# A gated mix of sliding-window attention and a mixer MLP on one Trainium2 core: the probabilities' block split in two, tokens loaded a unit earlier, five MLP steps moved ahead of the last P times V, and weight loads moved into the attention's end

## The chip, the core and the metric

The kernel runs on one NeuronCore of one Trainium2 chip. A core has five engines, each with an instruction queue of its own that it works off in order: TensorE (PE; its weight loads are shown apart as PEld), VectorE (DVE), ScalarE (ACT), GpSimd (POOL) and SyncE (SP). SP only issues DMAs here, and ACT issues some too. The engines meet at semaphores. Matmuls write PSUM, which has eight banks of 2 KB a partition; everything else lives in SBUF (128 partitions) or in HBM.

The metric is the device time of one execution in microseconds (us), the median of several runs. An execution's profile shows the span from the first to the last instruction of the program, which is about 2 us less.

## What is computed

`x` is (2048, 512), float32. Two branches are mixed by a gate of one number per token:

```python
g = _sigmoid((x * gate_w).sum(-1, keepdims=True))
# A: attention, H = 32 heads of 16, causal, window W = 256
q, k, v = split(x @ wqkv)
scores = jnp.einsum("bhqd,bhkd->bhqk", q, k) * (Dh ** -0.5)
mask = (idx[:, None] - idx[None, :] >= 0) & (idx[:, None] - idx[None, :] < W)
p = _softmax(jnp.where(mask, scores, -1e9), axis=-1)
a = einsum("bhqk,bhkd->bhqd", p, v) @ wo
# B: per-token MLP, F = 1792
y = _layernorm(x)
b = _gelu(y @ w1 + b1) @ w2 + b2
out = g * a + (1 - g) * b
```

The products are made in three terms from a high and a low part of each operand (`split`, `lo_part`), so each float32 weight block is loaded raw, copied to its high part and subtracted to get its low part: one copy on ACT or DVE and one subtraction on DVE or POOL.

## The kernel before

There are three stages, each one stream of work on PE with the other engines beside it. Nothing is scheduled by a planner while it runs: the order is written out, by a table of units in the first stage, by a string of 1,202 letters in the second, by a loop in the third. `tick` counts steps, and `after(k, fn)` emits `fn` k steps later; what is emitted earlier stands earlier in its engine's queue. A tile takes one of the buffers of its tag, and an instruction waits until the buffer's last user is done.

**Stage 1: projections (0 to about 149 us).** 48 units, each a matmul group of 12: Q or K of a head group for 512 tokens (`qk_unit`, L290) or V of 128 tokens (`v_unit`, L320). `at(n, fn)` puts other work ahead of unit n's matmuls. Q and K go through HBM: `qk_out` stores their high and low parts from `t` tiles, `load_stacks` (L331) loads the score operands of four heads into `qk`. `gaps` (L203) fills rows of the HBM copy. `stat_unit(i)` loads 128 tokens from `xa` (L441); after 3 steps ACT makes their sums (`sums`, L444 and L445), after 4 DVE makes the gate's dot product (`dot`, L448). `s_pair` (S; L344) makes a block of scores for the row maximum, two heads at a time; DVE masks it (L353) and reduces it (L354). In this stage two PSUM buffers (`ps_x`) are kept for it. The first ten blocks of queries are done here, two pairs a block. The pool `work` holds, in order of first use, `gws` and `waste` (2 KB a partition each), four `wv` (4 KB) and fourteen `t` (2 KB).

**Stage 2: attention, with MLP1 in its gaps (about 149 to 498 us).** `work` is closed and opened again on the same bytes. Its first tile is the block `five` of probabilities (tag `p`, L596); nine `t` follow. `p_tile` hands out seven slots in turn: five in this block, two in tiles of the pool `x`. Eight passes of four heads run over 16 blocks of 128 keys. The string `ORDER` gives the steps: T is `st_pair` (L399, scores of two heads; L401, the exponential on ACT, written to a slot; L403, masks on POOL), S is `s_pair` for the row maximum of what comes later, P is `pv` (L418, probabilities times V for 256 queries; the result is copied out by ACT or DVE at L425 and stored), and f is `fill`: one step of `mlp1_unit`, two matmuls (L621). A unit of MLP1 has 24 steps; there are 28 units, 672 steps, and the string has 647. Its result is copied out by ACT and stored to `hp`. Four PSUM banks `b0` to `b3` go round among T, S and P, one of them held by the open MLP1 unit. `block(p, kb)` runs at each first T of a key block and issues loads; in the last pass it starts the load and split of the first W2 blocks (`early_w2`) and of the first two tiles of MLP1's result (`load_h`).

After the string, the gelus of the two early tiles go to ACT, the last P is run, the pools are opened again (44 `t`), and a loop works off the MLP1 steps that are left.

**Stage 3: MLP2 and the attention's output (about 504 us to the end).** For each 512 tokens and each of 14 blocks of F, `mlp2` makes 12 matmuls (L832). `load_w2` (L650) and `load_h` (L674) run six items ahead; gelu is at L677, its high part at L681. At item 4 of the first 512 tokens, `attn_out` starts: it loads the row sums `su` (L783), takes their reciprocal on DVE (L788), stores them, loads the unscaled attention and the factors (L795, L796), scales (L799) and multiplies by Wo (L811; `load_wo`, L656).

Of the kernel before, what the change touches and what calls it, by code (L numbers as in the profile page):

```python
# [20 lines left out]
D = 512  # L21
# [6 lines left out]
C = 512  # L28
# [27 lines left out]
def gated_mix_kernel(ctx, tc: tile.TileContext, xt, x2, wq0, wqk, wv, wo, xa, gw, w1, w2, b1, b2, out):  # L56
    nc = tc.nc
    dve, act, pool, pe, sp = nc.vector, nc.scalar, nc.gpsimd, nc.tensor, nc.sync
# [5 lines left out]
    def nm(s):  # L64
        uid[0] += 1
        return f"{s}_{uid[0]}"
# [10 lines left out]
    def get(key, tag, bufs, shape, dt=F32):  # L77
        return left[key].tile(list(shape), dt, name=nm(tag), tag=tag, bufs=bufs)
# [3 lines left out]
    def t2(dt=F32, shape=(128, 512)):  # L82
        return get("work", "t", nt[0], shape, dt)
# [19 lines left out]
    def two():  # L103
        if not ring:
            return ps("x", (128, 2, 512))
        ring.append(ring.pop(0))
        return ps(ring[-1], (128, 2, 512))

    def small(tag, bufs, shape, dt=F32):
        return consts.tile(list(shape), dt, name=nm(tag), tag=tag, bufs=bufs)  # L110

    def view(t, *ap, off=0):
        return bass.AP(tensor=t.tensor, offset=t.offset + off, ap=[list(x) for x in ap])

    def f32(t):
        return t.bitcast(F32)

    def lo_part(lo, src, hi, eng=dve):
        eng.tensor_tensor(out=lo, in0=src, in1=f32(hi), op=ALU.subtract)  # L119
# [7 lines left out]
    def after(k, fn):  # L127
        todo.setdefault(step[0] + k, []).append(fn)
# [43 lines left out]
    def x8():  # L172
        return get("x", "x8", 10, (128, 2048), F32R)
# [4 lines left out]
    def split(w, raw, both=False):  # L178
        if both:
            dve.tensor_copy(w[:, 0], raw)  # L180
        else:
            copy(w[:, 0], raw)
        lo_part(w[:, 1], raw, w[:, 0])
# [142 lines left out]
    def load_stacks(p, a, n):  # L326
        g, j = divmod(p, 2)
        held_cols[p] = a + n
        for t in (1, 0):
            src = view(qkd[g, t], [S, 98], [100 * S, 2], [1, n], off=4 * j * 50 * S + a)  # L330
            sp.dma_start(f32(qk[14:112, 2 * t:2 * t + 2, a:a + n]), f32(src))  # L331
# [3 lines left out]
    def s_pair(p, qb, pr):  # L335
        if qb == 0 and pr == 0:
            mxs[p] = small("mx", 2, (128, 2, 2, NB))
        assert qb * 128 < held_cols[p]
        n = min(qb + 1, 3) * 128
        t0 = qb * 128 + 128 - n  # L340
        o = two()
        for e in range(2):
            r, k = ((0, 62), (64, 112))[e]
            pe.matmul(o[:, e, :n], qs[pr][r:k, qb * 128:qb * 128 + 128], ks[pr][r:k, t0:t0 + n],  # L344
                      start=True, stop=True)
        m = mxs[p][:, pr, :, qb]
        if qb < 2:
            for e in range(2):
                sc = small("scr", 2, (128, 256), BF16)
                dve.tensor_tensor_reduce(out=sc[:, :n], in0=o[:, e, :n], in1=wide[:, 256 - n:], scale=1.0, scalar=NEG,  # L350
                                         op0=ALU.add, op1=ALU.max, accum_out=m[:, e:e + 1])
        else:
            dve.copy_predicated(o[:, :, :128], tri, o[:, :, 256:384])  # L353
            dve.tensor_reduce(m, o[:, :, :256], mybir.AxisListType.X, ALU.max)  # L354
        if pr and qb % 4 == 3:
            put_max(p, qb - 3)
# [82 lines left out]
    def stat_unit(i):  # L439
        s = t2()  # L440
        sp.dma_start(s, xa[i])  # L441

        def sums():
            act.activation(waste, s, AF.Copy, scale=-1.0 / D, accum_out=mv[:, i, 0:1])  # L444
            act.activation(waste, s, AF.Square, bias=mv[:, i, 0:1], accum_out=mv[:, i, 1:2])  # L445

        def dot():
            dve.scalar_tensor_tensor(out=s, in0=s, scalar=1.0, in1=gws, op0=ALU.mult, op1=ALU.mult,  # L448
                                     accum_out=z[:, i:i + 1])

        after(3, sums)
        after(4, dot)

    def stat_end(half):
        ve = small("ve", 2, (128, NB // 2))
# [92 lines left out]
    def at(n, fn):  # L548
        plan.setdefault(n, []).append(fn)
# [5 lines left out]
    for i in range(4):  # L555
        at((3, 5, 6, 8)[i], lambda i=i: pool.memset(vs[:, 4 * i:4 * i + 4], 1.0))
    at(2, masks)
    at(10, load_consts)
    for g in range(NG):
        at((8, 16, 20, 24)[g], lambda g=g: gaps(g))  # L560
    for c in range(NCH):
        at((11, 20, 29, 44)[c], lambda c=c: load_stacks(0, c * C, C))
    for i in range(NB):
        at(10 + i, lambda i=i: stat_unit(i))
    at(21, lambda: stat_end(0))
    at(29, lambda: stat_end(1))
    at(25, lambda: load_mr(0))
# [6 lines left out]
    at(38, lambda: load_w1(0, dve))  # L574
    at(41, lambda: load_w1(1, dve))
    for qb in range(NB - LAG):
        at((17, 19, 21, 23, 25, 27, 29, 31, 34, 37)[qb], lambda qb=qb: [s_pair(0, qb, pr) for pr in range(2)])
    for n, u in enumerate(units):
        if n > 1:
            tick()  # L580
# [12 lines left out]
    extra = [f32(x8())[:, :1536].rearrange("p (h n) -> p h n", h=4) for _ in range(2)]  # L593
    np_ = [0]

    five = get("work", "p", 1, (128, 5, 4, 384))  # L596

    def p_tile():
        n = np_[0] % 7
        np_[0] += 1  # L600
        return extra[n // 4] if n in (2, 5) else five[:, n - n // 3]

    late = []

# [38 lines left out]
    def load_w2(f):  # L643
        if f % 2 == 0:
            w2t.append(x8())
            if f == 2:
                spare.append(x8())
        w = w2s[f] = w2t[-1][:, f % 2 * 2 * C:f % 2 * 2 * C + 2 * C].rearrange("p (k n) -> p k n", k=2)
        raw = t2()
        sp.dma_start(raw, w2[f])  # L650
        return lambda both=False: split(w, raw, both)

    def load_wo(dt):
        w, raw = wt(), t2()
        wos[dt] = w
        sp.dma_start(raw, wo[dt])  # L656
        return lambda both=False: split(w, raw, both)

    def early_w2():
        for n in range(4):  # L660
            def go(n=n):
                fn = load_w2(n)
                after(2, lambda: fn(True))
            after(1 + n, go)

    def early_wo(a):
        fns = [load_wo(a), load_wo(a + 1)]
        after(4, lambda: [fn() for fn in fns])

    hs = {}  # L670

    def load_h(c, f):
        s = t2()
        sp.dma_start(s, hp[c, f])  # L674

        def gelu():
            act.activation(s, s, AF.Gelu_apprx_tanh, bias=b1s[:, f:f + 1])  # L677

        def parts(dst=None):
            h, l = dst or (t2(F32R), t2(F32R))  # L680
            dve.tensor_copy(h, s)  # L681
            lo_part(l, s, h)
            hs[c, f] = h, l

        return gelu, parts
# [10 lines left out]
    def block(p, kb):  # L696
        tick()
        if kb % 2 == 0:
            if kb and p + 1 < 8:
                load_stacks(p + 1, kb * 128 - 256, 256)  # L700
            if not kb and p:
                load_stacks(p, S - 256, 256)
        if p in (0, 2, 4) and kb % 2 == 0:
            double(p // 2 + 1, kb // 4, 1 - kb // 2 % 2)
        if p == 7 and kb == LAG:
            early_w2()
        if p == 7 and kb == 12:
            early.extend(load_h(0, f) for f in range(2))

    early = []  # L710
    spot[0] = 0
# [4 lines left out]
    def run(order):  # L716
        for a in order:
            spot[0] += 1
            for fn in soons.pop(spot[0], []):
                fn()  # L720
            flush()
            if a == "T":
                p, kb, pr = lt.pop(0)
                if not pr:
                    block(p, kb)
                st_pair(p, kb, pr)
            elif a == "S":
                s_pair(*ls.pop(0))
            elif a == "P":
                pv(*lp.pop(0), not ls)  # L730
            else:
                fill()

    run(ORDER)
    flush()
    for f, (gelu, _) in enumerate(early):
        gelu()
# [17 lines left out]
    waiting = {}  # L755
    for f in range(2, 4):
        waiting[0, f] = load_h(0, f)
    for f in range(4, 6):
        waiting["w", f] = load_w2(f)
    for f in range(4, 6):  # L760
        waiting[0, f] = load_h(0, f)
    for f in range(4, 6):
        waiting.pop(("w", f))()
    while jobs or cur[0]:
        fill()
    flush()
# [3 lines left out]
    low, high = {"o0": 1, "o1": 1, "a4": 1, "a5": 1}, {f"a{i}": 1 for i in range(4)}  # L770
    open_psum(*((low, high) if "b0" in used else (high, low)))
    b2s = get("work", "b2s", 1, (128, D))
    sp.dma_start(b2s, view(b2, [0, 128], [1, D]))

    after(1, gate)
    for n in range(2):
        after(1 + 2 * n, lambda n=n: early_wo(2 * n))
    us = {}

    def attn_out(c):  # L780
# [64 lines left out]
    for n in range(len(seq)):  # L845
        tick()
        for k in (n + 6,):
            c, f = item(k)
            if f >= 0:
                if c == 0 and f > 3:  # L850
                    waiting["w", f] = load_w2(f)
                waiting[c, f] = load_h(c, f)
        c, f = item(n + 1)
        if ("w", f) in waiting and c == 0:
            waiting.pop(("w", f))()
        if (c, f) in waiting:
            waiting[c, f][1]()
        if item(n + 2) in waiting:
            waiting[item(n + 2)][0]()
        c, f = seq[n]  # L860
        if f == (4 if c == 0 else 2):
            attn_out(c)
        mlp2(c, f)
# [49 lines left out]
```

## Time and profile before

| what | us |
|---|---|
| three runs | 708.22, 712.19, 714.32 |
| median | 712.19 |
| profiled execution, its own time | 709.97 |
| its span | 708.0 |
| TensorE busy in it | 690.4 |

The page's first part gives, for each engine, busy time, share of the span and instructions. The granted clock of TensorE is 0.998 of full speed over the span. The page's slices of the span show DMA busiest in the first stage (eight or nine tenths) and least at the very end.

The chain of waits, which follows the work that ended last back to what released it, is PE for 78% of the span and DMA for 9%. Its DMA part is made of a few pieces, among them loads of tokens (`t<-in_xa`, 3%).

In the rows that follow, a timeline row has the start, the duration, the engine (with a q where its queue issues a DMA), the line, the operation, output and inputs with their shapes, the count, and in brackets the idle time before it and what ended that.

### The profile page before, as it was taken

The page shows a single profiled execution, that of the slowest core. Times are in us where ns is not written, and L with a number is a line of the kernel's source. Part 1 is how long each engine was busy: PE and PEld are TensorE (multiplying, and loading weights), DVE is VectorE, ACT ScalarE, POOL GpSimd, SP SyncE. Part 2 cuts the span into 40 slices and gives each one's busy share as a digit, 9 for nine tenths or more (in the row PEclk, how much of TensorE's full clock was granted, in tenths as well). Part 3 has the DMA queues.
Part 4 walks back from the last instruction along what each step waited for, and adds up shares of the span by engine and source line. Part 5 has one row for each costly group of instructions (what it writes and reads, how often), then busy time and mean ns, then how long its engine had stood idle before and what let it go on. Part 6 is the DMA issues. An engine that isn't in the chain of part 4 may idle for free.

```text
span 708.0 us, 16057 instructions
## 1 busy us (share of the span) xinstructions
PE 690.4 (98%) x5740; PEld 537.9 (76%) x5740; DVE 476.1 (67%) x964; ACT 388.3 (55%) x645; POOL 267.2 (38%) x623
## 2 busy tenths in 40 slices
PE   9999989979999999999999999999999999999997
PEld 6887767867777776777787777776777788888886
DVE  7626598947887787768678687784555745645554
ACT  6447453437767676677776867767633414124131
POOL 9600056316557574655665656658000000000000
PEclk9999999999999999999999999999999999999999
DMA  8998897766656666746776655524865544442531
GB/s 319 338 314 241 254 264 224 230 216 191 210 167 205 186 213 205 227 151 194 218 218 202 211 160 159 180 78 166 265 219 152 179 134 138 160 138 97 192 113 59
DMA packets 102534, 137.93 MB, mean 195 GB/s; under 512 B 13912, under 2 KB 53528, under 8 KB 102328
## 3 DMA queue, kind: packets, MB, share of 16 engines
q1 hardware_dynamic: 97848, 128.79, 57.8%
q10 hardware_dynamic: 4608, 8.13, 3.5%
q8 instruction: 46, 0.75, 0.4%
q14 instruction: 32, 0.26, 0.1%
HBM read 81.53 MB, written 54.30 MB: 192 GB/s over the span
## 4 chain that ended last, share of the span: by engine, by line
PE 78%; DMA 9%; SPq 4%; DVE 3%; ACT 2%; issue 2%; ACTq 0%; POOL 0%; DVEq 0%
PE ps_b L621 21%; PE ps_a L832 16%; PE ps_b L418 12%; PE ps_d L290 7%; PE ps_b L399 7%; PE ps_b L344 6%; PE ps_o L811 5%; PE ps_d L320 3%; DMA t<-in_xa 3%; DMA hp<-t 1%; SPq L795 1%; SPq L796 1%; ACT t L122 1%; PE ps_d L277 1%; DVE us L837 1%
## 5 line engine op out<-in xcount | busy, mean ns | idle before, releaser
L621 PE MATMUL ps_b<-x,w 64*128 64x512 f32 x1344 | 214.1, 397 | 0.7 <-DVE mx L354 0.4
L403 POOL TENSOR_SCALAR_AFFINE_SELECT p<-p 128x256 f32<-128x256 f32 x344 | 131.8, 411 | 108.1 <-ACT p L401 105.3
L401 ACT ACTIVATE p<-ps_b 128x768 f32<-128x768 f32 (+2 forms) x184 | 138.0, 770 | 47.8 <-PE ps_b L399 33.3
L832 PE MATMUL ps_a<-x,t 128*128 128x512 f32 x648 | 150.7, 390 | 1.6 <-DVE t L681 1.6
L354 DVE TENSOR_REDUCE mx<-ps_b 128x2 f32<-128x512 f32 x208 | 144.1, 693 | 7.1
L832 PEld LDWEIGHTS ps_a<-x,t 128*128 128x128 f32 x648 | 121.3, 188 | 28.3 <-issue 1.8
L621 PEld LDWEIGHTS ps_b<-x,w 64*128 64x128 f32 x1344 | 130.8, 187 | 12.3 <-issue 3.0
L353 DVE COPY_PREDICATED ps_b<-tri,ps_b 128x256 f32<-128x256 uint8 x208 | 88.3, 425 | 55.7 <-PE ps_b L344 42.1
L399 PE MATMUL ps_b<-qk 50*128 50x384 f32 (+5 forms) x512 | 91.2, 344 | 4.7 <-ACT p L401 3.8
L344 PE MATMUL ps_b<-qk 62*128 62x384 f32 (+3 forms) x472 | 85.7, 346 | 0.9 <-DMA qk<-qk 0.8
L290 PE MATMUL ps_d<-x,w 128*128 128x512 f32 x360 | 85.7, 392 | 0.0
L290 PEld LDWEIGHTS ps_d<-x,w 128*128 128x128 f32 x360 | 67.0, 188 | 15.2 <-issue 1.3
L418 PE MATMUL ps_b<-p,v 128*32 128x256 f32 (+1 forms) x1376 | 74.4, 329 | 0.8 <-ACT p L401 0.7
L122 ACT ACTIVATE t<-ps_b 128x512 f32<-128x512 f32 (+1 forms) x112 | 51.8, 490 | 37.8 <-PE ps_b L418 32.9
L399 PEld LDWEIGHTS ps_b<-qk 64*128 64x128 f32 (+1 forms) x512 | 51.9, 185 | 24.9 <-issue 6.0
L403 POOL TENSOR_SCALAR_AFFINE_SELECT x<-x 128x256 f32<-128x256 f32 x136 | 51.8, 408 | 35.8 <-ACT x L401 35.5
L401 ACT ACTIVATE x<-ps_b 128x768 f32<-128x768 f32 (+2 forms) x72 | 55.1, 777 | 17.2 <-PE ps_b L399 14.4
L344 PEld LDWEIGHTS ps_b<-qk 62*128 62x128 f32 (+1 forms) x472 | 46.8, 185 | 17.2 <-issue 4.8
L418 PEld LDWEIGHTS ps_b<-p,v 128*32 128x32 f32 x1376 | 38.9, 109 | 26.4 <-ACT p L401 4.3
L119 DVE TENSOR_TENSOR t<-t,t 128x512 fp32r<-128x512 f32 x70 | 48.5, 692 | 14.6 <-ACT t L122 11.6
L122 ACT ACTIVATE t<-t 128x512 fp32r<-128x512 f32 x16 | 10.1, 632 | 81.1 <-DVE t L799 43.5
L677 ACT ACTIVATE t<-t,b1s 128x512 f32<-128x512 f32 x56 | 38.0, 716 | 24.6 <-DMA t<-hp 23.9
(83 smaller groups left out, 676.1 us busy)
## 6 DMA issues: line engine op xcount, KB each, us to landing
qk<-qk SPq DMA_DIRECT2D x112, 196.0 KB
t<-hp SPq DMA_DIRECT2D x56, 256.0 KB
hp<-t SPq DMA_DIRECT2D x52, 256.0 KB
qk<-t SPq DMA_DIRECT2D x48, 256.0 KB
osc<-t SPq DMA_DIRECT2D x31, 256.0 KB
t<-in_w SPq DMA_DIRECT2D x28, 256.0 KB
w<-w SPq DMA_DIRECT2D x28, 256.0 KB
qk<-t ACTq DMA_DIRECT2D x24, 256.0 KB
```

The source lines that it names most:

```text
L119: eng.tensor_tensor(out=lo, in0=src, in1=f32(hi), op=ALU.subtract)
L122: act.activation(dst, src, AF.Copy)
L290: pe.matmul(o, a[:, dt * 128:(dt + 1) * 128], b[:, dt * C:(dt + 1) * C], start=n == 0, stop=n == 11)
L344: pe.matmul(o[:, e, :n], qs[pr][r:k, qb * 128:qb * 128 + 128], ks[pr][r:k, t0:t0 + n], start=True, stop=True)
L353: dve.copy_predicated(o[:, :, :128], tri, o[:, :, 256:384])
L354: dve.tensor_reduce(m, o[:, :, :256], mybir.AxisListType.X, ALU.max)
L399: pe.matmul(o[:, e, :w], ks[pr][r:k, kb * 128:kb * 128 + 128], qs[pr][r:k, kb * 128:kb * 128 + w], start=True, stop=True)
L401: act.activation(pt[:, :, :w], o[:, :, :w], AF.Exp, scale=0.25)
L403: pool.affine_select(out=pt[:, :, a:a + 128], in_=pt[:, :, a:a + 128], pattern=[[0, 2], [sgn, 128]], base=b, channel_multiplier=-sgn, comp ...
L418: pe.matmul(a[32 * h:32 * h + 32, at:at + w], vs[:, kb, v:v + 32], pts[p, kb][:, h, fr:fr + w], start=n == 0, stop=n == len(parts) - 1, sk ...
L621: pe.matmul(o[:, e], w[kt // 4][r:r + 64, k, m:m + 128], y[r:r + 64, a:a + C], start=n == 0, stop=n == 23)
L832: pe.matmul(accs[c][b], x[:, b * 128:(b + 1) * 128], w, start=f == 0 and n == 0, stop=f == FT - 1 and n == 2)
```

## The change

Five edits:

1. The block `five` becomes two tiles of three and two slots, opened one after the other. The order in which the seven slots are handed out stays the same.
2. `load_consts` and all token loads (`stat_unit`) go one unit sooner; the sums and dots come one step later after their load, and so stay at their units.
3. The first ten blocks of `s_pair` get other units: the first six one unit sooner, the seventh as before, the last three one unit later (the eighth 31 to 32, the ninth 34 to 35, the tenth 37 to 38). The load of the second 512 columns of score operands goes from unit 20 to 19.
4. Five f are added to the end of `ORDER`, ahead of the last P; the loop behind it has five fewer to do.
5. `early_w2` loads six W2 blocks and no longer four; the first two Wo blocks are loaded at key block 13 of the last pass and split two steps later. The loads that stood for them after the attention fall away, the other two Wo blocks are loaded at the third stage's first step, and `b2` two steps after that.

```diff
-        after(3, sums)
-        after(4, dot)
+        after(4, sums)
+        after(5, dot)
...
-    at(10, load_consts)
+    at(9, load_consts)
...
-        at((11, 20, 29, 44)[c], lambda c=c: load_stacks(0, c * C, C))
+        at((11, 19, 29, 44)[c], lambda c=c: load_stacks(0, c * C, C))
     for i in range(NB):
-        at(10 + i, lambda i=i: stat_unit(i))
+        at(9 + i, lambda i=i: stat_unit(i))
...
     for qb in range(NB - LAG):
-        at((17, 19, 21, 23, 25, 27, 29, 31, 34, 37)[qb], lambda qb=qb: [s_pair(0, qb, pr) for pr in range(2)])
+        at((16, 18, 20, 22, 24, 26, 29, 32, 35, 38)[qb], lambda qb=qb: [s_pair(0, qb, pr) for pr in range(2)])
...
-    five = get("work", "p", 1, (128, 5, 4, 384))
+    slots = [get("work", "p3", 1, (128, 3, 4, 384)), get("work", "p2", 1, (128, 2, 4, 384))]
+    slots = [slots[0][:, 0], slots[0][:, 1], extra[0], slots[0][:, 2], slots[1][:, 0], extra[1], slots[1][:, 1]]
 
     def p_tile():
-        n = np_[0] % 7
         np_[0] += 1
-        return extra[n // 4] if n in (2, 5) else five[:, n - n // 3]
+        return slots[(np_[0] - 1) % 7]
...
     def early_w2():
-        for n in range(4):
+        for n in range(6):
             def go(n=n):
                 fn = load_w2(n)
                 after(2, lambda: fn(True))
             after(1 + n, go)
 
-    def early_wo(a):
+    def early_wo(a, k):
         fns = [load_wo(a), load_wo(a + 1)]
-        after(4, lambda: [fn() for fn in fns])
+        after(k, lambda: [fn() for fn in fns])
...
         if p == 7 and kb == 12:
             early.extend(load_h(0, f) for f in range(2))
+        if p == 7 and kb == 13:
+            early_wo(0, 2)
...
-    run(ORDER)
+    run(ORDER + 5 * "f")
...
-    for f in range(4, 6):
-        waiting["w", f] = load_w2(f)
     for f in range(4, 6):
         waiting[0, f] = load_h(0, f)
-    for f in range(4, 6):
-        waiting.pop(("w", f))()
...
-    sp.dma_start(b2s, view(b2, [0, 128], [1, D]))
 
     after(1, gate)
-    for n in range(2):
-        after(1 + 2 * n, lambda n=n: early_wo(2 * n))
+    after(1, lambda: early_wo(2, 4))
+    after(3, lambda: sp.dma_start(b2s, view(b2, [0, 128], [1, D])))
...
-                if c == 0 and f > 3:
+                if c == 0 and f > 5:
                     waiting["w", f] = load_w2(f)
```

## The prediction

> **What bounds the kernel now.** I read the page first, then the busy time of three stages, then the list of TensorE's waits, and last the timeline around each of those waits. TensorE (PE) is busy nearly throughout; no other engine is near it.
>
> ```profile
> PE 690.4 (98%) x5740; PEld 537.9 (76%) x5740; DVE 476.1 (67%) x964; ACT 388.3 (55%) x645; POOL 267.2 (38%) x623
> ```
>
> The stage view (stage, its length, then busy time and count for each engine, granted clock, DMA share, GB/s) is cut where the first score product for the exponentials and the first MLP1 step after the last P times V begin. The wait view gives total, times, longest.
>
> ```profile
> 0.00:148.66 148.66, 144.17 (x629) 112.22 (x630) 105.37 (x192) 74.57 (x161) 59.14 (x71) 1.00 0.86 272
> 148.66:497.50 348.84, 341.85 (x4199) 259.49 (x4198) 254.54 (x573) 247.20 (x379) 208.08 (x552) 1.00 0.60 186
> 497.50:708.00 210.50, 204.35 (x918) 166.19 (x914) 116.18 (x199) 66.55 (x106) 0.00 (x0) 1.00 0.48 154
> PE ps_b L399 <- ACT p L401: 3.8, 1, 3.8
> PE ps_x L344 <- DVE mx L354: 2.7, 4, 0.9
> PE ps_o L811 <- ACT t L122: 0.6, 2, 0.4
> ```
>
> PE is idle for 4.5, 7.0 and 6.2 us in the three stages. The change leaves the number of matmuls as it is, so it can only win from those 17.6 us and from stretches at a lower clock. It pays where it removes a PE wait, and nowhere else.
>
> **Part 1, the exponentials' block in two parts.** The longest wait is a single one, just after the attention opens:
>
> ```profile
> 146.09 3.60 SPq L301 DMA_DIRECT2D qk<-t  x2
> 150.34 1.09 PE L621 MATMUL ps_b<-x,w 64*128 64x512 f32 x8
> 154.35 0.81 ACT L401 ACTIVATE p<-ps_b 128x768 f32<-128x768 f32 x1 [4.98 <-DMA t<-in_w]
> 155.21 0.45 PE L399 MATMUL ps_b<-qk 64*128 64x384 f32 x2 [3.77 <-ACT p L401]
> ...
> DMA  7899988896589999999999720000000007877039
> ...
> 151.43:155.21 3.78, 0.01 (x3) 0.00 (x1) 0.71 (x2) 0.81 (x1) 0.00 (x0) 1.00 0.79 293
> 155.74:159.15 3.41, 3.41 (x20) 2.81 (x18) 1.97 (x4) 1.58 (x2) 1.41 (x5) 0.50 0.00 0
> ```
>
> PE has done its eight matmuls by 151.43 and then waits 3.77 us for a bank that the first exponential must empty. That exponential waited 4.98 us on ACT, for a DMA. The DMA line (40 slices of 0.625 us from 140) is full up to about 152.5 and then empty: what it waits for is the tail of those transfers. Why does an exponential wait for a DMA at all? It writes `p`, 5x4x384x4 = 30,720 bytes a partition, the first tile of a newly opened pool. In order of first use the pool before held `gws` and `waste` (2 KB each), four `wv` (4 KB each), then `t` (2 KB each): 20,480 bytes, and then `t`. So `p` covers exactly the first five `t`, and some of those are still being read by the last stores of Q and K, issued from 146.09 on. The row names an MLP1 weight load as releaser, but that is only the last DMA on a shared semaphore; the stores fit the memory.
>
> With the block in two, the first tile has 18,432 bytes and ends inside the fourth `wv`. `gws`, `waste` and `wv` have no DMA left. The second tile, which does lie over `t`, is first written eight exponentials later in the order string, well after 154.35. So the first exponential starts when ACT is free, 154.35-4.98 = 149.4, and ends at 150.2, before PE asks for the bank at 151.43. That gives 3.77 us. The stall has a tail: from 155.74 the granted clock is 0.50 for 3.41 us with PE busy throughout, worth 3.41x0.5 = 1.7 us. **Together 5.5 us.** Below nothing is excluded: the new tiles lie on the same bytes and carry no operation more. Next late would be loads for the scores, and I see none due in those microseconds.
>
> [...]
>
> **Part 2, tokens a unit sooner and the row-maximum products moved.** The first stage's 2.7 us are four waits of the maximum's score products (`s_pair`, S) for a bank, since VectorE (DVE) hadn't reduced the pair before:
>
> ```profile
> 91.39 0.44 PE L344 MATMUL ps_x<-qk 62*128 62x384 f32 x2 [0.85 <-DVE mx L354]
> 92.45 0.44 PE L344 MATMUL ps_x<-qk 62*128 62x384 f32 x2 [0.62 <-DVE mx L354]
> 99.18 0.45 PE L344 MATMUL ps_x<-qk 62*128 62x384 f32 x2 [0.63 <-DVE mx L354]
> 100.24 0.44 PE L344 MATMUL ps_x<-qk 62*128 62x384 f32 x2 [0.62 <-DVE mx L354]
> ...
> 89.47 0.69 DVE L448 SCALAR_TENSOR_TENSOR t<-t,gws 128x512 f32<-128x512 f32 x1 [3.98 <-ACT waste L445]
> 91.61 0.69 DVE L354 TENSOR_REDUCE mx<-ps_x 128x2 f32<-128x512 f32 x1
> 99.41 0.69 DVE L354 TENSOR_REDUCE mx<-ps_x 128x2 f32<-128x512 f32 x1
> ...
> ACT waste L444 <- DMA t<-in_xa: 14.7, 5, 4.4
> ...
> 40.23 0.87 SPq L331 DMA_DIRECT2D qk<-qk  x2
> 52.96 0.44 PE L344 MATMUL ps_x<-qk 62*128 62x128 f32 x4
> 67.93 1.73 SPq L331 DMA_DIRECT2D qk<-qk  x2
> 74.97 2.88 PE L290 MATMUL ps_d<-x,w 128*128 128x512 f32 x12
> 77.78 0.61 PE L344 MATMUL ps_x<-qk 62*128 62x384 f32 x4
> ```
>
> S at unit 29 (91.39) finds both banks held by S of unit 27, whose reductions stand on DVE behind a gate dot that sat 3.98 us waiting for ACT's sums, and ACT waits 14.7 us in all for tokens. The new table puts that S at unit 26. In DVE's queue it is then ahead of the dot of unit 27, so both banks are free long before unit 29: 0.85+0.62. The next S goes from unit 31 to 32. A unit is 77.78-74.97 = 2.8 us, so PE asks at about 98.6+2.8 = 101.4 and the last reduction of the pair before ended at 100.1: 0.63+0.62. Tokens are loaded a unit sooner while sums and dots keep their units; ACT's waits shrink by up to 2.8 us each, which by itself is worth nothing, since ACT isn't what PE waits for. Each token tile is held a unit longer, one more of 14 buffers up to unit 24. The three last S, moved a unit back, bring DVE nothing more in sum.
>
> What it may cost: S for blocks 0 and 4 is now asked for at units 16 and 24, at about 50.2 and 75.0, while the operand loads `load_stacks` can only move a little. The first pair is issued at 40.23 and showed no wait at 52.96, so it lands within 12.7 us; behind one more token load it is issued at about 40.7, and the wait is between 0 and 3.2 us. The second pair is issued a unit sooner, now ahead of the two gap copies, at 65.1 to 66.5, lands within 9.9 us, and PE waits between 0 and 1.4 us. These are the far ends; no row shows the landing itself. The stores issued from 146.09 on were done by 154.35, so 8.3 us is the longest landing that the rows bear out rather than allow; by it the first pair is there at 49.0 and the second by 74.8, both just in time. I take 0.5 us for the two. **2.7-0.5 = 2.2 us.**
>
> **Part 3, the last P times V, and the loads at the attention's end.**
>
> ```profile
> 486.54 0.94 SPq L674 DMA_DIRECT2D t<-hp  x2
> 489.50 0.62 DVE L180 CAST x<-t 128x512 fp32r<-128x512 f32 x1
> 490.15 0.77 DVE L119 TENSOR_TENSOR x<-t,x 128x512 fp32r<-128x512 f32 x1
> 492.96 0.43 DVE L425 COPY t<-ps_b 128x256 f32<-128x256 f32 x1 [2.03 <-PE ps_b L418]
> 495.06 0.42 DVE L425 COPY t<-ps_b 128x256 f32<-128x256 f32 x1 [1.68 <-PE ps_b L418]
> 495.36 0.66 ACT L401 ACTIVATE p<-ps_b 128x256 f32<-128x256 f32 x2 [0.73 <-PE ps_b L399]
> 496.07 0.64 PE L418 MATMUL ps_b<-p,v 128*32 128x256 f32 x8 [0.70 <-ACT p L401]
> 497.50 6.36 PE L621 MATMUL ps_b<-x,w 64*128 64x512 f32 x50
> 498.04 0.91 SPq L650 DMA_DIRECT2D t<-in_w  x2
> 502.10 1.15 ACT L122 ACTIVATE x<-t 128x512 fp32r<-128x512 f32 x2 [3.44 <-DMA t<-in_w]
> 522.57 0.95 DVE L788 RECIPROCAL su<-su 128x128 f32<-128x128 f32 x1 [5.10 <-DMA su<-osc]
> 524.55 8.64 PE L832 MATMUL ps_a<-x,t 128*128 128x512 f32 x36 [1.41 <-DVE t L681]
> ```
>
> The last P waits 0.70 us until the last exponentials end (495.36+0.66 = 496.02). Five MLP1 steps (two matmuls each; 50 matmuls in 6.36 us, so 0.25 us a step) are work taken from the loop that follows and put under this wait: 1.27 us of cover for 0.70. They finish one MLP1 unit and start the next, whose bank is the P product's before, copied out from 495.06 on. **0.7 us.** Below nothing: P could wait for its own bank, but that is one of the exponentials'.
>
> Two more W2 blocks are loaded and split before the end. Each split costs DVE 0.62+0.77 = 1.4 us; they come ahead of the two copies at 492.96 and 495.06, where DVE idles 2.03 and 1.68 us. They fit, by 0.3 us for the second. Their loads go into SP's queue after the pair of 486.54, where it has nothing else to issue before the copy of 492.96 lets an output store go. A load lands at most 502.10-498.04 = 4.1 us after its issue in a busier stretch, so by about 491.5. Two Wo blocks follow. Their two copies on ACT (1.15 us) stand in front of the last exponentials, where ACT idles 0.73: these end at most 0.4 us later, at 496.4, and P isn't reached before 495.37+1.27 = 496.6. **Nothing, with 0.2 us to spare.** Without that cover the price is one load's landing, 4 us.
>
> What it buys: in the last stage ACT no longer waits 3.44 us for W2 before the last MLP1 copies, and four of the loads, and b2, leave SP's queue ahead of the row sums' load `su`. The reciprocal waited 5.10 us for it, in front of the casts that PE then waited 1.41 for; `attn_out` after it waited 0.6. Between 0 and 2.0; the transfers are taken away, not only moved, so I take 1.41 and a third of 0.6: **1.6 us.**
>
> **The sum.** 5.5+2.2+0.7+1.6 = 10.0 us, all on PE's path. The profiled execution took 709.97 (span 708.0 and 1.97 around it), so 700.0. The three runs (708.22, 712.19, 714.32) have their median 2.2 above the profile; the mean of all four is 711.2, 1.2 above. I forecast 700.0+1.2 = **701**.
>
> **Rivals.**
> - The half clock isn't there in most timed runs: then Part 1 brings 3.8, not 5.5, and the time is 703. For: it is one row of one execution. [...] 0.12.
> - The S products, asked for sooner, wait for their operands: the 2.2 aren't won and up to 3.2+1.4 are lost, 711.2-7.8+4.6 = 708, more likely about 706. For: the first stage's DMA share is 0.86. 0.12.
> - The split doesn't do what it says: the first exponential waits for some other transfer that ends at the same time; 4.5 us remain, 707. For: the releaser that the row names. Against: the exponential reads no such load. 0.07.
> - Slower: the nine `t` buffers run out in the last pass. Place: blocks 11 to 15, where two W2 blocks, two h tiles, two Wo blocks and a P accumulator are held at once. If a load must wait for a buffer until the split before it is done, each link costs 4.1+1.4 = 5.5 us, with P's copies on DVE and the last exponentials on ACT queued behind. One link is paid for by Parts 1 and 2 (7.7 us); from the second on it decides: 11.0 and 1.7 for the clock against 7.7 is 711.2+5.0 = 716, with three 722. Against: I count at most eight of nine. 0.09.
>
> **How the numbers follow.** The forecast has 0.60; its own range is 698 to 705. About 1% (7 us here, 705.1) is what a measurement of this kernel can tell from no change. Faster by more: nearly all of the forecast, most of the clock's rival, a little of the next two, 0.66. Within 1%: 0.25. Slower: 0.09. The range runs from 697 (all of 5.5+2.7+0.7+2.0 = 10.9 us won, 700.3, and the 3 us by which the runs lie around their mean) to 709, which takes in both middle rivals and leaves out the slower one.
>
> **What would show it.** Part 1: ACT's first exponential within 1 us of the copy before it, no PE wait over 0.5 us between 145 and 160, no stretch at 0.50. Part 2: no S product waiting for a reduction; token waits of ACT clearly under 14.7; if wrong, a wait of S for `qk<-qk`. Part 3: the last P without a wait, no wait of ACT for a W2 load, the reciprocal's 5.10 gone. A wait of DVE or ACT for a load between 485 and 500 would show the slower rival. The forecast is wrong if the 5.5 us are still there or come back as another wait within the next pass.

## The result and the profile after

| | before | after |
|---|---|---|
| median of 6 runs, us | 712.30 (708.22 to 715.28) | 702.09 (699.39 to 706.80) |
| ratio, 95% interval | | 0.9865 (0.982 to 0.991) |
| profiled execution, its span | 708.0 | 697.6 |
| both kernels again, on another chip than e1 to e4, median | 711.86 (11 runs) | 702.67 (6 runs), ratio 0.9885 (0.984 to 0.993) |

The change makes the kernel 1.2 to 1.4% faster. The forecast of 701 is 1.1 below the first median and 1.7 below the second. One run of the kernel before, at 718.75 us, fell in a slower state of the chip and is left out of every mean below. The page's engine line of the changed kernel:

```profile
PE 687.5 (99%) x5740; PEld 537.2 (77%) x5740; DVE 473.1 (68%) x966; ACT 386.5 (55%) x643; POOL 269.9 (39%) x623
```

The list of TensorE's waits, of 0.2 us and up, without the one of the warm-up products at the start (total, times, longest):

```profile
PE ps_x L344 <- DVE mx L350: 1.4, 1, 1.4
PE ps_x L344 <- DVE mx L354: 1.1, 2, 0.6
PE ps_b L399 <- DMA qk<-md: 0.9, 2, 0.7
PE ps_b L418 <- POOL p L403: 0.4, 1, 0.4
PE ps_b L399 <- DVE mx L354: 0.3, 1, 0.3
PE ps_a L829 <- DVE t L681: 0.2, 1, 0.2
PE ps_b L621 <- ACT p L401: 0.2, 1, 0.2
```

The 3.8 us for the first exponential are gone, and so is the last P's 0.7. The maximum's products (`ps_x`) still wait, 2.5 us in all, and one P waits for GpSimd, which none did.

Both profiles cut by the same three events:

| from | to | before | after | gain |
|---|---|---|---|---|
| start | first score product of the exponentials | 148.66 | 148.07 | 0.6 |
| that | first MLP2 product | 355.13 | 348.78 | 6.3 |
| that | end | 204.26 | 200.76 | 3.5 |

So the sum of the terms, 10.0, stands beside 10.4, but two of its three parts don't: 2.2 were forecast for the first stage and 1.6 for the start of MLP2 (for the stretch between them 6.2). The boundary of stages 1 and 2 in the timeline and in windows of the changed kernel (length, busy time of PE, PEld, DVE, ACT, POOL, granted clock, DMA share, GB/s):

```profile
148.67 0.80 ACT L401 ACTIVATE p<-ps_b 128x768 f32<-128x768 f32 x1
...
144.00:152.00 8.00, 7.92 (x53) 6.19 (x53) 3.59 (x8) 2.71 (x4) 0.82 (x3) 1.00 0.96 275
152.00:156.00 4.00, 4.00 (x42) 3.85 (x40) 3.77 (x7) 2.71 (x4) 3.13 (x10) 1.00 0.99 347
```

ACT goes to the first exponential with no idle time, PE is busy for 11.92 of 12 us, and the clock stays at 1.00. The DMA share shows the loads behind it going on as well.

### The profile page after: what moved, and what is told of

Same layout as the page of the kernel before. It is cut to its first block, busy times and chain, and to the rows that moved or that the text cites. A ratio compares the mean times of both kernels' runs of the same rounds, so it can differ in the third digit from the quotient of the medians.

```text
span 697.6 us, 16045 instructions
## 1 busy us (share of the span) xinstructions
PE 687.5 (99%) x5740; PEld 537.2 (77%) x5740; DVE 473.1 (68%) x966; ACT 386.5 (55%) x643; POOL 269.9 (39%) x623
## 4 chain that ended last, share of the span: by engine, by line
PE 80%; DMA 8%; DVE 3%; POOL 2%; issue 2%; ACT 2%; SPq 2%; ACTq 0%; DVEq 0%; POOLq 0%
PE ps_b L621 22%; PE ps_a L829 21%; PE ps_b L418 11%; PE ps_b L399 7%; PE ps_b L344 6%; PE ps_o L808 6%; PE ps_d L290 4%; PE ps_d L320 2%; DMA v<-in_xt 2%; DMA md<-ms 1%; DMA qk<-qk 1%; DMA qk<-md 1%; DMA gws<-in_gw 1%; DVE us L834 1%; DMA wv<-in_wq 1%
## 5 line engine op out<-in xcount | busy, mean ns | idle before, releaser
L403 POOL TENSOR_SCALAR_AFFINE_SELECT p<-p 128x256 f32<-128x256 f32 x344 | 134.0, 419 | 99.6 <-ACT p L401 99.0
L399 PE MATMUL ps_b<-qk 64*128 64x384 f32 (+5 forms) x512 | 91.1, 343 | 1.2 <-DMA qk<-md 0.9
```

The costliest lines, as they stand in the source:

```text
L399: pe.matmul(o[:, e, :w], ks[pr][r:k, kb * 128:kb * 128 + 128], qs[pr][r:k, kb * 128:kb * 128 + w], start=True, stop=True)
L403: pool.affine_select(out=pt[:, :, a:a + 128], in_=pt[:, :, a:a + 128], pattern=[[0, 2], [sgn, 128]], base=b, channel_multiplier=-sgn, comp ...
```

## The experiments

Each run's span comes with its mean granted clock. Where many runs are spoken of, the mean of span x (1 - clock) over them is called the loss to the clock, and the mean of span x clock the rest. The loss is an upper bound, since it also counts time in which PE would have stood at full clock too (see e2). Single profiles differ by 3 us and more in waits that no edit is near (see e7), so a term under 1 us is read from the wait itself and not from the time.

### One part alone on the kernel before

**e1_split**: the two tiles of the block and nothing else.

```diff
-    five = get("work", "p", 1, (128, 5, 4, 384))
+    slots = [get("work", "p3", 1, (128, 3, 4, 384)), get("work", "p2", 1, (128, 2, 4, 384))]
```

> The kernel before with the exponentials' block in two parts, and nothing else of the change. Theory A (the gains are separable, and this is the largest): no wait of PE over 0.5 us between 145 and 160, no stretch at a granted clock of 0.50, first score product to the last P times V shorter by 5.5 us, ratio 0.992 (about 706.5 beside a median of 712.3). Rival B (the half clock is in few timed runs): the profile as in A, but the ratio at 0.9947 (3.8 us). Rival C (the stall went because the loads came otherwise, not because of the block's place): the wait of about 3.8 us is still there and the ratio is 1.00.

Measured: 706.65 beside 712.06, ratio 0.9915 (0.989 to 0.994). There is no wait for the first exponential and no half clock after it; the profile has one stretch at 0.50, from 102.16, behind waits of the first stage. Theory A holds, in size too: 5.4 us.

**e2_stage1**: constants, tokens, sums, stack load and table of the first stage, and nothing else.

```diff
-        at(10 + i, lambda i=i: stat_unit(i))
+        at(9 + i, lambda i=i: stat_unit(i))
...
-        at((17, 19, 21, 23, 25, 27, 29, 31, 34, 37)[qb], lambda qb=qb: [s_pair(0, qb, pr) for pr in range(2)])
+        at((16, 18, 20, 22, 24, 26, 29, 32, 35, 38)[qb], lambda qb=qb: [s_pair(0, qb, pr) for pr in range(2)])
```

> The kernel before with the first stage's edits alone: constants, tokens and their sums a unit sooner in loading, the second stack load a unit sooner, the new table of the row maximum's products. Theory A (the four old waits, 2.7 us, are exchanged for new ones of 2.4 us): first score product of the exponentials 0.3 to 0.9 us earlier than 148.66, new waits of PE for the row maximum at about 57.7 and 119 to 121, the wait of 3.8 us for the first exponential unchanged, ratio 0.999. Rival B (the predicted 2.2 us are won and the profile of the changed kernel was an odd execution): first stage at 146.5, ratio 0.997.

Measured: 710.91, ratio 0.9968 (0.994 to 0.999), 12 runs. The ratio is B's (between the means, 1.3 us), the profile is A's: 3.6 us of waits for the maximum, more than the 2.7 of before. The wait at the boundary is 4.4 us. The first two rows are the wait list, the others windows of this profile: the new wait at unit 38, what follows it, the boundary's wait, what follows that.

```profile
PE ps_b L399 <- ACT p L401: 4.4, 1, 4.4
PE ps_x L344 <- DVE mx L354: 3.6, 4, 1.9
...
118.89:122.30 3.41, 0.89 (x5) 0.43 (x4) 3.34 (x6) 1.12 (x2) 1.80 (x2) 1.00 0.73 220
122.30:125.71 3.41, 3.41 (x10) 2.60 (x9) 3.41 (x3) 0.63 (x1) 2.96 (x2) 0.50 0.28 90
153.02:156.43 3.41, 1.16 (x12) 0.64 (x8) 1.83 (x4) 0.00 (x0) 0.00 (x0) 1.00 0.98 322
156.43:163.26 6.83, 4.67 (x24) 4.02 (x26) 2.25 (x4) 2.43 (x3) 2.26 (x6) 0.50 0.23 81
```

Behind the two waits at unit 38, 1.90 and 0.62 us, the clock stood at 0.50 as well: for 3.41 us with PE busy throughout, worth 1.7 by the prediction's reckoning (half of PE's busy time there). Behind the boundary's wait it is 6.83 us here, where the profile that the prediction used showed 3.41. It begins while PE still stands, and PE is busy for 4.67 of it, so by that reckoning it is worth 2.3 us beyond the wait, not half of 6.83.

**e3_five**: five more MLP1 steps ahead of the last P.

```diff
-    run(ORDER)
+    run(ORDER + 5 * "f")
```

> The kernel before with five more MLP1 steps ahead of the last P times V, and nothing else. Theory A: the last P's wait of 0.70 us is gone and no other takes its place, 0.7 us, ratio 0.999. Rival B (the wait only moves, to the MLP1 unit that then starts in the bank of the P product before, or the later stage gives it back): within 0.2 us of the kernel before, ratio 1.000.

Measured: 710.75, ratio 0.9975 (0.995 to 1.000). The last P's wait is gone from the list and none is in its place. From the end of the last P to MLP2 it is 4.71 us in place of 6.22, which is 1.27 for five steps moved and 0.24 more. A, as far as so small a term can be told.

**e4_loads**: six W2 and two Wo blocks early, `b2` later.

```diff
-        for n in range(4):
+        for n in range(6):
...
+        if p == 7 and kb == 13:
+            early_wo(0, 2)
...
-    for n in range(2):
-        after(1 + 2 * n, lambda n=n: early_wo(2 * n))
+    after(1, lambda: early_wo(2, 4))
+    after(3, lambda: sp.dma_start(b2s, view(b2, [0, 128], [1, D])))
```

> The kernel before with the loads alone: six W2 blocks and two Wo blocks in the attention's end, b2 three steps later. Theory A (the last stage's gain comes from the loads taken out of its beginning): first MLP2 product to the end 3.2 to 3.8 us shorter than 204.2; the masks of the last exponentials slower than before, since VectorE splits W2 beside them, and a P times V that waits, which costs 0.5 to 1.2 us; in all 2.5 us, ratio 0.9965. Rival B (it needs the five MLP1 steps too, since these let VectorE cast ahead): the last stage gains no more than 1.6 us, in all 0.5 us, ratio 0.999. Rival C (the loads compete with the attention's end and ACT or VectorE waits there for one): slower by 2 us or more, ratio 1.003.

Measured: 710.90, ratio 0.9990 (0.996 to 1.002). From MLP2 to the end it takes 201.64 (the loads' old place later on is taken out as well, in lines not shown). The two masked P are as in the changed kernel, and the last P waits 0.70, as in the kernel before. The expectation's 204.2 was the wrong measure: with the old loads the same stretch is 202.52 in e1_split and 202.25 in e3_five (first rows), with the new ones 201.64 here and 200.76 in the changed kernel (last rows).

```profile
502.36:704.88 202.52, 197.99 (x866) 161.46 (x864) 112.54 (x193) 63.70 (x102) 0.00 (x0) 1.00 0.47 151
507.96:710.21 202.25, 197.88 (x866) 161.47 (x864) 113.44 (x194) 64.14 (x102) 0.00 (x0) 1.00 0.47 152
```

```profile
506.33:707.97 201.64, 197.38 (x866) 161.70 (x864) 110.23 (x186) 62.38 (x99) 0.00 (x0) 1.00 0.46 148
496.85:697.61 200.76, 196.71 (x866) 161.93 (x864) 110.08 (x187) 61.50 (x98) 0.00 (x0) 1.00 0.46 148
```

So the loads bring 0.6 to 0.9 us alone. With the five steps it is about 1.4: the stretch takes 202.4 us on average in e1, e2, e3 and e9, which have the old loads, and 201.0 in the changed kernel, e5 to e8, e10 and e11. Some 1.9 of the first comparison's 3.5 belonged to that one execution of the kernel before. For the last stage rival B comes nearer than A; why the loads alone fall short of 1.4 stays open.

### The changed kernel again, and with other tables

**e5_after**: the changed kernel itself.

> The changed kernel itself once more, as the measure for the next runs. Theory A (in the timed runs the kernel before loses more to the reduced clock than its profile showed): mean granted clock 0.998 to 1.000 in nearly all runs, against 0.992 to 0.995 in most runs of the kernel before, that is about 3 us of the 10; first MLP2 product to the end 200.5 to 201.5, since 204.2 in the first profile of before was a long one (202.0 to 202.7 in four others with that code or part of it). Rival B (the clock is the same for both, the 10 us are waits alone): clock under 0.996 in half of the runs. Ratio 0.9865 for both.

Measured: 702.67, ratio 0.9885. Of 60 runs of the kernel before, 47 had a clock of 0.995 or less; of 12 of the changed kernel, 2 had. The loss to the clock is 3.75 us before and 1.23 after, so up to 2.5 of the gain are the clock; the rest went from 706.1 to 700.0. MLP2 to the end took 200.78. A.

**e6_oldtable**: the old table and stack load, all else as in the changed kernel.

```diff
-        at((11, 19, 29, 44)[c], lambda c=c: load_stacks(0, c * C, C))
+        at((11, 20, 29, 44)[c], lambda c=c: load_stacks(0, c * C, C))
...
-        at((16, 18, 20, 22, 24, 26, 29, 32, 35, 38)[qb], lambda qb=qb: [s_pair(0, qb, pr) for pr in range(2)])
+        at((17, 19, 21, 23, 25, 27, 29, 31, 34, 37)[qb], lambda qb=qb: [s_pair(0, qb, pr) for pr in range(2)])
```

> The changed kernel with the old table of the row maximum's products and the old stack load; tokens stay a unit sooner. Theory A (the new table exchanges waits for others of the same length, tokens sooner do nothing for PE): four or five waits of PE for the maximum, 2.5 to 3.1 us, around 91 and 100; time within 0.7 us of the changed kernel's, but for runs where the clock falls to 0.50 after 102, which take 1.7 us more. Rival B (the table brings the predicted 2.2 us): 2 us slower than the changed kernel. Rival C (tokens sooner alone clear the gate dots, so the old waits go without the table): waits under 1.5 us.

Measured: 703.43, ratio 0.9886 (0.986 to 0.992), beside 702.67. One burst of waits for the maximum, 3.1 us, with a half clock behind it:

```profile
93.33 0.45 PE L344 MATMUL ps_x<-qk 62*128 62x384 f32 x2 [2.46 <-DVE mx L354]
94.39 0.49 PE L344 MATMUL ps_x<-qk 62*128 62x384 f32 x2 [0.62 <-DVE mx L354]
...
91.23:94.64 3.41, 0.69 (x4) 0.43 (x4) 3.24 (x7) 2.78 (x8) 2.48 (x3) 1.00 0.59 187
94.64:98.05 3.41, 3.41 (x10) 2.56 (x9) 3.41 (x8) 2.54 (x8) 0.79 (x1) 0.50 0.75 214
```

A: between the means the new table is worth 0.4 us, which can't be told from nothing, and tokens sooner don't clear the old waits.

**e7_table**: the changed kernel with another table.

```diff
-        at((16, 18, 20, 22, 24, 26, 29, 32, 35, 38)[qb], lambda qb=qb: [s_pair(0, qb, pr) for pr in range(2)])
+        at((17, 19, 20, 22, 24, 26, 28, 31, 34, 37)[qb], lambda qb=qb: [s_pair(0, qb, pr) for pr in range(2)])
```

> The changed kernel with another table: 17, 19, 20, 22, 24, 26, 28, 31, 34, 37. Theory A (what counts is that the reductions of the pair before are ahead of a unit's other VectorE work when the next pair asks): PE's waits for the maximum under 0.7 us in all, first score product of the exponentials at 145.8 to 146.6, 1.7 us faster than the changed kernel. Rival B (VectorE is full in units 26 to 40, with GpSimd's operations beside it, and any table only moves the waits): they come back with 2 us or more at other units, time as the changed kernel's.

Measured: 705.07, ratio 0.9911 (0.988 to 0.994). The waits for the maximum fell to 1.4 us, all of it at unit 20, one unit behind the pair before. But the first score product came at 147.92, and the attention had waits for its loads that no edit here is near:

```profile
PE ps_b L344 <- DMA qk<-qk: 3.0, 3, 1.7
PE ps_b L399 <- DMA qk<-md: 2.2, 2, 1.6
PE ps_x L344 <- DVE mx L350: 1.4, 2, 1.1
```

Neither theory: the waits shrank, the time didn't. These `qk` loads made PE wait 0.9 us in the changed kernel's first profile and 2.7 in its second (1.7 and 1.0). Whether the table plays a part in the 5.2 here stays open.

### The tail, the boundary and a better table

**e8_tail**: two of the five steps ahead of the last P but one.

```diff
-    run(ORDER + 5 * "f")
+    run(ORDER[:-3] + "ff" + ORDER[-3:] + "fff")
```

> The changed kernel with two of the five MLP1 steps ahead of the last P times V but one, three ahead of the last. Theory A (that P waits because its masks on GpSimd take 2.84 us in place of 2.19 beside VectorE's splits, and the last has more cover than it needs): both P without a wait over 0.2 us, 0.6 us faster than the changed kernel in the stretch from the first score product of the exponentials to the first MLP2 product. Rival B (the wait moves to the last P, whose exponentials then end later than PE asks): a wait of 0.5 us or more there, no gain.

Measured: 703.58, ratio 0.9889 (0.985 to 0.993), beside 702.67. No P waits for GpSimd any more; one of 0.17 us for ACT is left, and the last P has none. A for the wait; 0.6 us can't be told in the time.

**e9_first**: the five-slot block whole, but the two score tiles outside it in turns 0 and 3.

```diff
-        return extra[n // 4] if n in (2, 5) else five[:, n - n // 3]
+        return extra[n // 3] if n in (0, 3) else five[:, n - 1 - n // 4]
```

> The kernel before, its block of five whole, but the two score tiles that lie outside the block take the first and the fourth turn instead of the third and the sixth. So the first two exponentials don't touch the block, the third, some 3.7 us later, does. Theory A (the wait is the block's memory, read by the last stores of Q and K until about 5.6 us after the copy before the first exponential): the first exponential has no idle time before it over 0.3 us, the third waits 0.5 to 2 us, PE's wait for ACT shrinks from 3.2 to 4.4 us to 0 to 1.5 us; 2.5 to 5 us faster than before, ratio 0.994. Rival B (the exponentials wait for a transfer that ends then, wherever they write): the first exponential waits 4 us or more, ratio 1.00.

Measured: 706.46, ratio 0.9920 (0.989 to 0.995). ACT in its timeline, with `x` for the tiles outside the block:

```profile
147.16 0.53 ACTq L301 DMA_DIRECT2D qk<-t  x1
149.25 0.60 ACT L122 ACTIVATE v<-ps_d 128x512 f32<-128x512 f32 x1 [2.12 <-PE ps_d L320]
149.74 0.80 ACT L401 ACTIVATE x<-ps_b 128x768 f32<-128x768 f32 x1
152.14 0.81 ACT L401 ACTIVATE x<-ps_b 128x768 f32<-128x768 f32 x1 [1.59 <-PE ps_b L399]
153.41 0.81 ACT L401 ACTIVATE p<-ps_b 128x768 f32<-128x768 f32 x1 [0.46 <-PE ps_b L399]
```

The same loads and stores run, and the first exponential doesn't wait, since it writes elsewhere. The third, the first to write the block, would have had to wait 0.5 to 2 us by the expectation and waits for PE alone: the stores must have been done by then. That takes rival B away, with it the prediction's third rival, and gives the split's gain without splitting anything.

**e10_nosplit**: the changed kernel with the block in one, the edit of e1_split taken back.

> The changed kernel with the exponentials' block in one part again. Theory A (the split is worth the same with the rest of the change as without it): PE's wait of 3.2 to 4.4 us for the first exponential is back, the clock at 0.50 for 3.4 to 6.8 us after it, 5.5 us slower than the changed kernel, ratio to before 0.995. Rival B (the first stage's edits end the stores sooner, so that the split is worth less now): the wait under 2 us, ratio 0.990.

Measured: 708.67, ratio 0.9955 (0.992 to 0.999); 6.0 us slower than e5_after, which ran on another chip, or 5.0 by the two ratios. Its timeline names a store of Q and K as the releaser, as Part 1 of the prediction has it:

```profile
156.04 0.81 ACT L401 ACTIVATE p<-ps_b 128x768 f32<-128x768 f32 x1 [4.32 <-DMA qk<-t]
```

PE waits 3.1 us and the profile's mean clock is 0.993, beside 1.00 in e5_after. A. Over all runs, the kernels with this wait (before, e2, e3, e4, e10) lose 3.8 to 4.3 us to the clock, those without it (e1, e5 to e9, e11) 0.4 to 2.6.

**e11_combo**: the edit of e8_tail and a third table.

```diff
-        at((16, 18, 20, 22, 24, 26, 29, 32, 35, 38)[qb], lambda qb=qb: [s_pair(0, qb, pr) for pr in range(2)])
+        at((16, 19, 21, 23, 25, 27, 30, 33, 36, 39)[qb], lambda qb=qb: [s_pair(0, qb, pr) for pr in range(2)])
```

> A try at a better one: the changed kernel with the steps of e8_tail and the table 16, 19, 21, 23, 25, 27, 30, 33, 36, 39. Theory A (the wait at unit 18 goes with the second pair a unit later, those at 30 to 39 with three units between pairs): waits of PE for the maximum under 1 us in all, against 1.65 to 2.87 in the changed kernel's profiles; first stage 1.5 us shorter, in all 2 us faster than the changed kernel, 700.5. Rival B (the sum stays, since VectorE has no more room): waits of 2 us or more, the same time. Waits of the attention's score products for their loads, 1.5 to 5 us in one execution, can hide either.

Measured: 700.61 (698.82 to 703.15), ratio 0.9827 (0.979 to 0.986). The waits for the maximum are 1.4 us, both at one block, and the loss to the clock is the least of all, 0.4 us. It is the fastest here, 2.1 us below the changed kernel's mean of 12 runs, with an uncertainty as large (95%: -0.1 to 4.2).

**e12_wo**: the split of the two early Wo blocks goes behind the last P.

```diff
-            early_wo(0, 2)
+            early_wo(0, 3)
```

> The changed kernel with the split of its two early Wo blocks one block step later, behind the last P times V. Theory A (VectorE's two-operand subtractions beside GpSimd slow the masks): the last two masks take 0.77 us in place of 1.42, the six before them, which stand beside a W2 split, still 2.84, and P times V still waits 0.4 for these. Rival B (the masks are slow for another reason): 1.42 still. PE's time the same within 0.5 us in this stretch.

Measured, in one run: 701.48. GpSimd's masks of the last block in the kernel before, in the changed kernel, and here, and in the changed kernel VectorE beside them:

```profile
492.94 2.19 POOL L403 TENSOR_SCALAR_AFFINE_SELECT p<-p 128x256 f32<-128x256 f32 x6
495.81 0.77 POOL L403 TENSOR_SCALAR_AFFINE_SELECT p<-p 128x256 f32<-128x256 f32 x2 [0.68 <-ACT p L401]
```

```profile
486.74 2.84 POOL L403 TENSOR_SCALAR_AFFINE_SELECT p<-p 128x256 f32<-128x256 f32 x6
489.78 1.42 POOL L403 TENSOR_SCALAR_AFFINE_SELECT p<-p 128x256 f32<-128x256 f32 x2 [0.20 <-ACT p L401]
...
487.10 0.77 DVE L119 TENSOR_TENSOR x<-t,x 128x512 fp32r<-128x512 f32 x1
489.35 1.58 DVE L119 TENSOR_TENSOR w<-t,w 128x512 fp32r<-128x512 f32 x2
```

```profile
487.64 2.84 POOL L403 TENSOR_SCALAR_AFFINE_SELECT p<-p 128x256 f32<-128x256 f32 x6
490.68 0.77 POOL L403 TENSOR_SCALAR_AFFINE_SELECT p<-p 128x256 f32<-128x256 f32 x2 [0.20 <-ACT p L401]
```

With the subtractions of Wo gone from beside them, the last two masks are back at 0.77; the six that still stand beside a W2 subtraction stay at 2.84. A.

## Why the prediction was right or wrong

**Part 1 (5.5 us): right in mechanism and size.** "`p` covers exactly the first five `t`, and some of those are still being read by the last stores of Q and K": e9 shows that the exponential is free as soon as it writes elsewhere, e10 that the wait comes back with the block. The first slot alone takes 4x384x4 = 6,144 bytes, which lie on `gws`, `waste` and the first `wv`; so the exponential waited for the block as a whole, not for the bytes that it writes. The size is 5.4 alone and 5.0 to 6.0 in the changed kernel. By the runs' means it is made of 2.8 us of waits at least and 2.7 of clock at most (e1: rest 703.4 beside 706.2, loss 1.1 beside 3.8), where the prediction had 3.77 and 1.7: the profile had one of the shorter half-clock tails. One reading was off without harm: the 22 full slices of the DMA line reach to 153.75, not 152.5, which is nearer still to the exponential's start at 154.35.

**The clock's rival (0.12) fell, and on the other side.** The half clock isn't rare in the timed runs: the kernel before loses more to it there, 3.75 us on average by the upper bound, than in the profile, 1.7. In that profile it stood behind 3.41 us in which PE was busy for 0.53 (152.33 to 155.74).

**Part 2 (2.2 us): the step that failed.** It said of the products at unit 26: "In DVE's queue it is then ahead of the dot of unit 27, so both banks are free long before unit 29", and of the last three: "moved a unit back, bring DVE nothing more in sum". The four old waits did go. What the step left out is that each product moved meets another place where VectorE is late:

```profile
57.72 0.83 PE L344 MATMUL ps_x<-qk 62*128 62x256 f32 x4 [1.38 <-DVE mx L350]
119.17 0.45 PE L344 MATMUL ps_x<-qk 62*128 62x384 f32 x2 [0.45 <-DVE mx L354]
120.23 0.44 PE L344 MATMUL ps_x<-qk 62*128 62x384 f32 x2 [0.62 <-DVE mx L354]
...
50.76 0.63 ACT L444 ACTIVATE waste<-t 128x512 f32<-128x512 f32 x1 [3.63 <-DMA qk<-t]
52.88 0.69 DVE L119 TENSOR_TENSOR w<-t,w 128x512 fp32r<-128x512 f32 x1 [4.42 <-ACT w L122]
115.59 0.69 DVE L119 TENSOR_TENSOR t<-ps_d,t 128x512 fp32r<-128x512 f32 x1 [2.85 <-POOL t L504]
```

The second block, now at unit 18, finds the first one's reductions behind a subtraction that waited 4.42 us for ACT, which had itself stood 3.63 us and went on right behind the issue of a store. The tenth, at unit 38, finds the ninth's behind operations that waited 2.85 us for GpSimd. In six profiles with the old table the waits for the maximum are 1.9 to 3.2 us, 2.8 on average; in six with the new one 1.0 to 3.6, 2.5 on average. The term is 0.3 by the waits, and 0.4 by the time in e6. Only e2's time says more, 1.3 us between the means with the tokens sooner as well, and what that would be beside the waits stays open. The prediction's own test, "no S product waiting for a reduction", failed. Its other test can mislead: the waits of ACT's sums that end with a token load fell from 14.7 to 5.6 us, but those with a store or another copy behind them are new, and all of ACT's idle time before the sums only went from 18.4 to 16.0. The rival that the products would wait for their operands fell: no profile of the changed kernel shows such a wait in the first stage.

**Part 3.** The last P's 0.7 is right (e3). "Nothing, with 0.2 us to spare" is right for what it priced: the last P doesn't wait, VectorE's wait for a W2 load (2.55 us at 476.58) delays nothing, and ACT's wait for Wo is 0.34 us. But it looked at VectorE's and ACT's queues and not at GpSimd's masks beside VectorE's subtractions (six of them took 2.84 us there and 2.19 in the kernel before). The P before the last finds its masks late; the kernel before, then the changed one:

```profile
494.60 0.40 PE L418 MATMUL ps_b<-p,v 128*32 128x128 f32 x8
```

```profile
487.76 0.39 PE L418 MATMUL ps_b<-p,v 128*32 128x128 f32 x4
488.55 0.41 PE L418 MATMUL ps_b<-p,v 128*32 128x128 f32 x4 [0.41 <-POOL p L403]
```

Eight products that ran in 0.40 us take 1.20 (487.76 to 488.96). In e8 they take 0.49, with a new wait of 0.17 shortly before.

For the start of MLP2 the 1.6 us is near the 1.4 that several profiles show, partly by luck. The 1.41 us of it, PE's wait for the cast behind the reciprocal, stand in the first profile alone: e1, e2, e3 and e9, with the same loads, have 0.27 at most there. The queue ahead of `su` was real. Counted from the first MLP2 product, its load is issued 12.2 to 12.9 us later with the old loads and 9.9 to 11.9 with the new, the reciprocal starts at 17.0 to 18.8 and at 14.8 to 16.6, and the first product with Wo at 27.6 to 29.4 and at 27.3 to 27.4. But the prediction expected the reciprocal's wait to be gone, and it is still there:

```profile
512.42 0.95 DVE L785 RECIPROCAL su<-su 128x128 f32<-128x128 f32 x1 [5.32 <-DMA su<-osc]
```

Of these 5.32 us, 4.3 pass between the issue at 508.10 and the reciprocal: most of the wait is the load's own way, and only the part in front of it could be taken away. ACT no longer waits 3.44 us for W2, as forecast.

**The sum.** 5.5 + 0.3 + 0.7 - 0.8 + 1.4 = 7.1 us by the runs' own sizes, beside 8.6 between the means of 60 and 12 runs (uncertain by 1.8). That the forecast's 10.0 comes so near to the profiles' 10.4 is in good part luck: the profile of before holds some 1.9 us in its last stage that other executions lack, and the changed kernel's profiled execution was the fastest of its 12. The rival of nine buffers running out, 0.09, left no trace.

## What to carry over

When a pool is opened again on used bytes, let its first tile lie on bytes whose last reader is long done, or give the first turn to a tile elsewhere (5.4 us in e1, a ratio of 0.9920 in e9). A wait that moved with a shared engine's backlog wasn't removed here by shifting the work that met it (2.8 us on average with the old table, 2.5 with the new): look up what the engine does at the new place before counting the old wait as won. Price a short PE gap with the clock that may fall behind it (2.7 us at most of the 5.4 in e1), and take the clock from many runs rather than one profile.

## What the runs showed of the hardware

**Half clocks and the stretches before them.** In e2_stage1 the two stretches at 0.50 begin at 122.30 and 156.43, 34.13 us apart, which is ten times the 3.41 us that the first of them lasts; the second lasts 6.83, two such lengths. The 3.41 us before each had PE busy for 0.89 and 1.16 us. In e1_split the 3.42 us before a stretch at 0.50 had 2.15 (first two rows), while in e7_table the full clock went on behind 3.41 us with 1.73 (last two rows). So PE's busy time before it didn't by itself tell whether the clock fell, and what else decides it isn't shown:

```profile
98.74:102.16 3.42, 2.15 (x10) 1.29 (x9) 3.35 (x7) 0.92 (x3) 2.69 (x10) 1.00 0.90 169
102.16:105.57 3.41, 3.41 (x9) 2.65 (x8) 3.11 (x7) 0.35 (x1) 2.15 (x5) 0.50 0.95 260
```

```profile
273.18:276.59 3.41, 1.73 (x18) 1.35 (x16) 1.50 (x4) 0.97 (x2) 1.90 (x6) 1.00 0.87 256
276.59:280.00 3.41, 3.41 (x58) 2.22 (x58) 3.03 (x7) 2.07 (x4) 0.41 (x1) 1.00 0.46 154
```

**GpSimd's masks took longer beside VectorE's subtractions**: 0.77 us for two alone (kernel before, 495.81), 1.42 beside two subtractions that read two tiles each (changed kernel, 489.78), with VectorE at 0.79 apiece (0.65 for the two at 503.08 of the same profile, where no mask runs). In e12, which takes the subtractions from beside them, the two masks took 0.77 again. How the subtractions slow the masks isn't shown.
